# Top-k attention and a SwiGLU block in fp32: the `w_val` product by seven quarter products, and the transposed exp kept in the buffer of exp

## The chip, the cores and the metric

The kernel runs on one core of a Trainium2 chip. The metric is the device time of one execution in microseconds; the figure of the kernel before is the median of three runs. One more execution was recorded by the hardware profiler, and every row below is from it.

Names used throughout: PE is the matmul engine (PEld its weight loads), DVE the vector engine, ACT the scalar engine, POOL the GpSimd engine, SP the engine that issues most DMAs. Each takes its instructions in order. SBUF is the on-chip memory, PSUM the banks that PE writes its results to.

## The reference

```python
# attention: q, k, v are (8, 8, 576, 64), all fp32
scores = scale * np.matmul(q, k.transpose(0, 1, 3, 2))
kth = np.partition(scores, -32, axis=-1)[..., -32:-31]
scores = np.where(scores >= kth, scores, -1e9)
scores = scores - np.max(scores, axis=-1, keepdims=True)
attn = np.exp(scores)
attn = attn / (np.sum(attn, axis=-1, keepdims=True) + 1e-9)
attn_out = np.matmul(attn, v)
# the heads side by side: x is (4608, 512)
x = attn_out.transpose(0, 2, 1, 3).reshape(4608, 512)
# w_gate, w_val: (512, 1536); w_out: (1536, 512)
g = x @ w_gate
out = (g / (1 + np.exp(-g)) * (x @ w_val)) @ w_out
```

## The kernel before

**Attention** goes in 160 units: for each of 8 batches, 5 tiles of queries (four of 128, the last of 64), and 4 pairs of heads. A unit of the first four tiles has two heads of 576 scores in each of 128 rows; in the last tile both heads share the rows, and a unit is half the work (128x576 instead of 128x1152). So a batch is 20 units, 16 full ones and 4 halves. One unit passes through these helpers:

- `scores` (L278): PE multiplies query and key into four PSUM banks (two for a half), ACT copies them to `sc` (L313, L299).
- `select` (L316): DVE finds the 32nd largest score by four rounds of `max` and three of `match_replace` (L329, L333), then writes a mask into `e` (L339).
- `penalize` (L343): POOL makes `bias` (L349) and adds `sc` to `e` (L351).
- `weigh` (L354): ACT's exp with the row sums (L360). `normalize` (L368): DVE's reciprocal, ACT scales `e` (L375).
- `turn` (L377): PE transposes `e` in nine 128x128 chunks into PSUM (L387), ACT copies them to a tile `et` (L388). `values` (L403): PE multiplies `et` with `v` (L407, L416), ACT copies the result to the block's `xT` (L431).

**The feed-forward part** goes in 18 blocks of 256 rows (`feed`, L457). A block has six pairs of chunks of 128 columns of `w_gate` and `w_val`. For a pair, `product` makes a gate product and a value product, each 2 chunks x 4 matmuls of 128x256 (L471) into one PSUM bank (`ps_f`, 3 buffers). After the gate, ACT makes tanh, half and add (L496 to L498) and POOL a product (L499); after the value, ACT copies (L503) and POOL multiplies into `h` (L504). Then the product with `w_out`: in block 0 as it stands (L517), in the others already by seven quarter products (`quarter`, L545; matmuls L557), for which POOL makes sums and differences of the quarters of `h` (L564, L572, L577, L605) and of the results (L543). Their weights `T[1]` to `T[7]` are made once by POOL, at the end of `weights` (L125).

**Weights** come in 36 pieces during the first 190 us, each rounded by ACT, DVE and POOL (`rounded`, L103).

**What sets the order.** The main loop (L729) is written out by hand. In step n it puts out, in this order: what is left on the queue `on_act`, `penalize(n-1)`, the queue `on_pool`, `turn(n-3)`, `values(n-4)`, the matmuls of `scores(n+1)`, `weigh(n-1)`, the copies of these scores, and DVE's rounds of `select(n)`, with pieces of the feed-forward part between them (`pieces`, L702). How many pieces a unit gets is a credit, `share(n)` (L689): `beside` (6.4) less what the unit's other PE work costs, in units of 4 matmuls of 128x256. `product` charges 2 a product, a `quarter` 1.5, so a block of seven quarter products costs 34.5. `product` does not emit its ACT part: it puts a function on `on_act`, which in turn puts one on `on_pool`; `piece` (L661) empties each as soon as it holds two, and the main loop at fixed places. The last lines (L793 on) bind PE, DVE, ACT and POOL to the order written; SP's DMAs are ordered by the scheduler. A block starts when all its rows of `xT` are done, and the last two blocks run when attention is over.

Of the kernel before, what the change touches and what calls it, by code (L numbers as in the profile page):

```python
# [9 lines left out]
ALU = mybir.AluOpType  # L10
FP32 = mybir.dt.float32
# [4 lines left out]
P = 128  # L16
# [4 lines left out]
BLK = 256  # L21
# [4 lines left out]
def kernel(  # L26
# [35 lines left out]


    nc = tc.nc
    B, H, S, D = q.shape
# [18 lines left out]
    conv = ctx.enter_context(tc.tile_pool(name="conv", bufs=2))  # L84
    ffn = ctx.enter_context(tc.tile_pool(name="ffn", bufs=2))
    ps_t = ctx.enter_context(tc.tile_pool(name="ps_t", bufs=5, space=PSUM))
    ps_f = ctx.enter_context(tc.tile_pool(name="ps_f", bufs=3, space=PSUM))

    ident = consts.tile([P, P], FP32, name="ident")
    make_identity(nc, ident[:])  # L90
    NV = 4
    vlast = []
# [32 lines left out]
    def weights():  # L125
# [66 lines left out]
        T[3] += [wo[:, MQ + m, hi] for m in range(MQ)]  # L192
        yield

    ready = [0]
    early = [lambda: None]
    plain_done = []
    T = {i: [] for i in range(1, 8)}
# [178 lines left out]
    def turn(n):  # L377

        last = units[n][1] == J
        e = state[n].pop("e")  # L380
        et = work.tile([P, 2 * J + 1, P], FP32, tag="et", name="et")
        for c0, cn in ((0, J), (J, 1)) if last else ((0, J), (J, 1), (J + 1, J)):
            ps = ps_t.tile([P, 512], FP32, tag="t", name="etps")
            kl = R if last and c0 == J else P
            for c in range(cn):
                k0 = (c0 + c) * P
                nc.tensor.transpose(ps[0:kl, c * P : (c + 1) * P], e[:, k0 : k0 + kl], ident[:])  # L387
            nc.scalar.copy(  # L388
                et[0:kl, c0 : c0 + cn, :],
                ps[0:kl, 0 : cn * P].rearrange("p (c j) -> p c j", c=cn),  # L390
            )
            if c0 == J:
                yield
        state[n]["et"] = et
# [62 lines left out]
    def feed(kb):  # L457
# [4 lines left out]
        x = xT.pop(kb)  # L462
        hs = []

        def product(w, s, then):
            ps = ps_f.tile([P, 2, BLK], FP32, tag="f", name="f")
            need(4 * s + (2 if w is wg else 4))
            for i in range(2):
# [11 lines left out]
                yield 1  # L480

        plain = kb == 0
        first, late = slice(0, P), slice(P, BLK)
# [5 lines left out]
        for s in range(MS):  # L489
            h = ffn.tile([P, 2, BLK], FP32, tag="h", name="h", bufs=MS + 1)  # L490
            hs.append(h)


            def gate(ps, h=h):
                half = ffn.tile([P, 2, BLK], FP32, tag="gv", name="half_g", bufs=3)
                nc.scalar.activation(h[:], ps[:], AF.Tanh, scale=0.5)  # L496
                nc.scalar.mul(half[:], ps[:], 0.5)
                nc.scalar.add(h[:], h[:], 1.0)  # L498
                on_pool.append(lambda: nc.gpsimd.tensor_mul(h[:], h[:], half[:]))  # L499

            def value(ps, h=h, s=s):
                val = ffn.tile([P, 2, BLK], FP32, tag="gv", name="val", bufs=3)
                nc.scalar.copy(val[:], ps[:])  # L503
                on_pool.append(lambda: nc.gpsimd.tensor_mul(h[:], h[:], val[:]))  # L504

            yield from product(wg, s, gate)
            yield from product(wv, s, value)
        o = ffn.tile([P, 2, DM], FP32, tag="o", name="o", bufs=1)
# [31 lines left out]
        x_ps = ps_f.tile([P, 2, DH], FP32, tag="f", name="x_ps")  # L540

        def tt(out, in0, in1):
            nc.gpsimd.tensor_tensor(out, in0, in1, ALU.add)  # L543

# [35 lines left out]
        yield from quarter(5, x_ps[:, 0])  # L580
        a = ffn.tile([P, 2, DH], FP32, tag="gv", name="p57", bufs=3)

# [4 lines left out]
        on_act.append(keep_x)  # L587
        b = ffn.tile([P, 2, DH], FP32, tag="gv", name="p16", bufs=3)

# [99 lines left out]
    def share(n):  # L689
# [8 lines left out]

        beside = 6.4 if T[1] else 7.0
        return beside * n_heads(units[n][1]) / 2 - others  # L700
# [136 lines left out]
```

## Time and profile before

| what | us |
|---|---|
| median of three runs | 1822.87 (1821.8 to 1823.49) |
| the profiled execution | 1821.36 |
| its span, first to last instruction | 1819.6 |
| PE busy | 1702.6 (94%) |
| DVE busy | 1603.0 (88%) |
| ACT busy | 1219.7 (67%) |
| POOL busy | 1036.1 (57%) |
| matmuls of the gate product, L471, 1728 records | 401.6, 382 ns each |
| matmuls of the value product, L471, 1728 records | 399.1, 382 ns each |
| POOL `e + sc`, L351, 160 | 382.8, 2393 ns each |
| POOL `h` products, L499 and L504, 108 each | 138.2 and 139.7 |
| DMA | 59.65 MB, mean 33 GB/s |

An fp32 matmul of the program stands in the trace as two records, one behind the other. The length of a record (382 ns) is longer than the distance at which such records follow each other, since matmuls are pipelined; rates are read from a run of records in the timeline. A wait in the profile is put down to what came last, and idle time of an engine that isn't the bottleneck costs nothing by itself.

### The profile page before, as it was taken

The numbers are of one execution on the slowest core, as the hardware profiler recorded it, in microseconds if no ns is written. First come the engines' busy times: TensorE is split into PE (matmuls) and PEld (weight loads), VectorE is DVE, ScalarE is ACT, GpSimd is POOL, SyncE is SP. The second block draws the span as 40 slices with busy tenths as digits, with TensorE's granted clock in tenths as the row PEclk, the third lists the DMA queues.
The fourth block names the chain that finished last, engine by engine and source line by source line (L and its number), as shares of the span: only waits on it lengthen the run. The fifth ranks groups of instructions, "written<-read, shape, count | busy, mean of one in ns | idle before, by whom it ended". The sixth has DMA issues, their size and how long they took to land.

```text
span 1819.6 us, 30520 instructions
## 1 busy us (share of the span) xinstructions
PE 1702.6 (94%) x10756; PEld 1406.1 (77%) x10756; DVE 1603.0 (88%) x3372; ACT 1219.7 (67%) x2977; POOL 1036.1 (57%) x930
## 2 busy tenths in 40 slices
PE   3447999899999999999999999999999999999999
PEld 2336768687788788887888878887888878888887
DVE  7999999999999799997999989998999989998400
ACT  6788666677667576666767676767676766675532
POOL 5878656555565646554465646564556554646354
PEclk7668999999999999999999999999999999999999
DMA  7433030002100030000300021000300011000000
GB/s 195 132 95 103 3 86 8 12 1 48 47 1 13 2 76 17 13 1 19 76 13 1 12 56 39 1 13 3 74 19 13 1 36 32 1 13 12 1 12 12
DMA packets 109305, 59.65 MB, mean 33 GB/s; under 512 B 88544, under 2 KB 96992, under 8 KB 109152
## 3 DMA queue, kind: packets, MB, share of 16 engines
q1 hardware_dynamic: 108016, 57.37, 12.1%
q8 instruction: 85, 1.39, 0.3%
q14 instruction: 68, 0.56, 0.1%
q10 hardware_dynamic: 1136, 0.33, 0.1%
HBM read 48.23 MB, written 9.44 MB: 32 GB/s over the span
## 4 chain that ended last, share of the span: by engine, by line
PE 88%; DVE 4%; ACT 4%; POOL 2%; issue 2%; DMA 1%; SPq 0%; POOLq 0%; DVEq 0%; ACTq 0%
PE f L471 42%; PE x_ps L557 9%; PE av L416 8%; PE etps L387 8%; PE s L308 8%; PE y_ps L557 7%; PE s L294 2%; DVE rest L333 2%; PE av L407 2%; DVE m L329 1%; PE o_ps L517 1%; PE kqps L263 1%; ACT e L360 1%; DVE e L339 1%; ACT e L375 1%
## 5 line engine op out<-in xcount | busy, mean ns | idle before, releaser
L329 DVE MAX8 m<-rest 128x8 f32<-128x576 f32 x864 | 612.7, 744 | 2.2
L351 POOL TENSOR_TENSOR e<-e,sc 128x1152 f32<-128x1152 f32 (+1 forms) x160 | 382.8, 2393 | 87.5 <-DVE e L339 73.1
L333 DVE MATCH_REPLACE8 rest<-m,rest 128x576 f32<-128x576 f32 x576 | 423.0, 739 | 0.0
L471 PE MATMUL f<-xT,wg 128*128 128x256 f32 x1728 | 401.6, 382 | 0.0
L471 PE MATMUL f<-xT,wv 128*128 128x256 f32 x1728 | 399.1, 382 | 0.0
L471 PEld LDWEIGHTS f<-xT,wg 128*128 128x128 f32 x1728 | 323.0, 190 | 62.8 <-issue 21.5
L471 PEld LDWEIGHTS f<-xT,wv 128*128 128x128 f32 x1728 | 324.4, 190 | 58.8 <-issue 16.6
L499 POOL TENSOR_TENSOR h<-h,half_g 128x512 f32<-128x512 f32 x108 | 138.2, 1279 | 293.6 <-ACT h L498 293.3
L329 DVE MAX8 m<-sc 128x8 f32<-128x576 f32 x288 | 205.0, 747 | 103.7 <-ACT sc L299 56.9
L360 ACT ACTIVATE e<-e,bias 128x576 f32<-128x576 f32 x288 | 222.1, 777 | 80.6 <-POOL e L351 80.5
L387 PE MATMUL etps<-ident,e 128*128 128x128 f32 (+1 forms) x1312 | 184.0, 285 | 90.9 <-issue 32.3
L388 ACT COPY et<-etps 128x512 f32<-128x512 f32 (+1 forms) x448 | 184.4, 484 | 124.6 <-PE etps L387 123.5
L387 PEld LDWEIGHTS etps<-ident,e 128*128 128x128 f32 (+1 forms) x1312 | 158.4, 146 | 118.0 <-issue 38.4
L504 POOL TENSOR_TENSOR h<-h,val 128x512 f32<-128x512 f32 x108 | 139.7, 1294 | 184.5 <-ACT val L503 184.4
L375 ACT ACTIVATE e<-e,tot 128x576 f32<-128x576 f32 x288 | 211.9, 790 | 1.5 <-DVE tot L372 1.5
L333 DVE MATCH_REPLACE8 rest<-m,sc 128x576 f32<-128x576 f32 x288 | 211.5, 740 | 0.0
L308 PE MATMUL s<-kqT 64*128 64x288 f32 x1024 | 172.3, 449 | 9.1 <-ACT kqT L268 8.8
L339 DVE TENSOR_SCALAR e<-sc,m 128x576 f32<-128x576 f32 x288 | 173.3, 637 | 3.4
L416 PE MATMUL av<-et,v 128*64 128x128 f32 (+1 forms) x2560 | 171.4, 279 | 0.0
L313 ACT COPY sc<-s 128x288 f32<-128x288 f32 x512 | 164.3, 403 | 2.5 <-PE s L308 2.5
L496 ACT ACTIVATE h<-f 128x512 f32<-128x512 f32 x108 | 65.4, 605 | 132.9 <-PE f L471 132.9
L416 PEld LDWEIGHTS av<-et,v 128*64 128x64 f32 x2560 | 134.9, 143 | 22.7 <-issue 6.8
(73 smaller groups left out, 2021.1 us busy)
## 6 DMA issues: line engine op xcount, KB each, us to landing
v<-in_v_dram SPq DMA_DIRECT2D x32, 256.0 KB, 3.0
kq_in<-in_k_dram SPq DMA_DIRECT2D x63, 128.0 KB, 2.8
kq_in<-in_q_dram SPq DMA_DIRECT2D x63, 128.0 KB, 2.9
w<-in_moe_w_gate_dram SPq DMA_DIRECT2D x12, 512.0 KB, 3.7
w<-in_moe_w_val_dram SPq DMA_DIRECT2D x12, 512.0 KB, 3.8
w<-in_moe_w_out_dram SPq DMA_DIRECT2D x12, 512.0 KB, 3.6
out_dram<-o SPq DMA_DIRECT2D x38, 128.0 KB, 2.4
out_dram<-o SPq DMA_DIRECT2D x16, 256.0 KB, 2.4
```

Of the source, the lines that this page charges most:

```text
L308: nc.tensor.matmul(ps[:, 0:half], slab[d, q0 : q0 + P], slab[d, k0 : k0 + half])
L329: nc.vector.max(m[:, t, 8 * r : 8 * r + 8], cur[:, hs])
L333: nc.vector.match_replace(rest[:, hs], m[:, t, 8 * r : 8 * r + 8], cur[:, hs], LOWEST)
L339: nc.vector.tensor_scalar(e[:, hs], sc[:, hs], m[:, t, TOP_K - 1 : TOP_K], FAR, ALU.is_lt, ALU.mult)
L351: nc.gpsimd.tensor_tensor(e[:, every], e[:, every], sc[:, every], ALU.add)
L360: nc.scalar.activation(e[:, hs], e[:, hs], AF.Exp, bias=bias[:, t : t + 1], scale=scale, accum_out=tot[:, t : t + 1],)
L375: nc.scalar.mul(e[:, hs], e[:, hs], tot[:, t : t + 1])
L387: nc.tensor.transpose(ps[0:kl, c * P : (c + 1) * P], e[:, k0 : k0 + kl], ident[:])
L388: nc.scalar.copy(et[0:kl, c0 : c0 + cn, :], ps[0:kl, 0 : cn * P].rearrange("p (c j) -> p c j", c=cn),)
L416: nc.tensor.matmul(av[hh * R : (hh + 1) * R, 0:ql], v_last[:, hh, :] if c == J else vt[:, hh, c, :], moving, start=last and c == 0, stop=c ...
L471: nc.tensor.matmul(ps[:, i, :], w[:, kc, m * P : (m + 1) * P], x[:, kc, :], start=(kc == 0), stop=(kc == KC - 1),)
L557: nc.tensor.matmul(ps, lhsT, T[i][m], start=m == 0, stop=m == MQ - 1)
```

## The change

1. **Value product.** In blocks 2 to 17 the value product of a pair of chunks goes by seven quarter products. `w_val` is cut in halves by rows (`c` 0-1 and 2-3) and by the two chunks of the pair, `x` in halves by rows and by its 256 columns. Each quarter product is two matmuls of 128x128. Four of them go into one PSUM tile (`f6157`), three into a second (`f234`). ACT copies both; POOL puts the four quarters of the result together by four additions (`sum_up`) and multiplies them into `h`. Block 0 and block 1 keep the old product.
2. **Sums of `x`.** At the start of a block POOL makes four differences `t1` to `t4` of the quarters of `x`.
3. **Sums of `w_val`.** They are made once, after block 1's value products, by POOL (four operations a pair; one of them overwrites a quarter of `wv`), written to DRAM (256 KB and 128 KB a pair), and read back for every pair of every block: `s12` has two buffers in SBUF, `s4` one. A fetch is issued for the pair after next (`s12`) or the next pair (`s4`).
4. **Transposed exp.** `turn` writes the transposed chunks back into the tile `e` that they were read from; the tile `et` is gone.
5. **Buffers and share.** `h` has 6 buffers (7 before), the tiles of the tag `gv` 4 (3 before). A quarter-product value costs 1.75 (2 before), and `beside` is 6.25 (6.4 before).

```diff
-    NV = 4
+    NV, NG = 4, 4
...
+        while not plain_v:
+            yield
+        for s in range(MS):
+            c0 = 2 * s * P
+            a11, a12 = (wv[:, i : i + 2, c0 : c0 + P] for i in (0, 2))
+            a21, a22 = (wv[:, i : i + 2, c0 + P : c0 + 2 * P] for i in (0, 2))
+            s12, s4 = sums_tiles()
+            nc.gpsimd.tensor_tensor(s12[:, 0], a21, a22, add)
+            nc.gpsimd.tensor_tensor(s12[:, 1], s12[:, 0], a11, sub)
+            nc.gpsimd.tensor_tensor(s4[:], a12, s12[:, 1], sub)
+            nc.gpsimd.tensor_tensor(a21, a11, a21, sub)
...
+            nc.sync.dma_start(kept[0][:], s12[:].rearrange("p a c m -> p (a c m)"))
+            nc.sync.dma_start(kept[1][:], s4[:].rearrange("p c m -> p (c m)"))
+            sv.append(kept)
+            yield
...
+    def fetch_s12(s):
+        t = ffn.tile([P, 2, 2, P], FP32, tag="s12", name="s12", bufs=2)
+        nc.sync.dma_start(t[:].rearrange("p a c m -> p (a c m)"), sv[s][0][:])
+        return t
...
-        et = work.tile([P, 2 * J + 1, P], FP32, tag="et", name="et")
+        et = e[:].rearrange("p (c j) -> p c j", j=P)
...
+        quick = kb >= 2
+        if quick:
+            while len(sv) < MS:
+                next(weight)
+            if not coming:
+                coming.extend([fetch_s12(0), fetch_s12(1)])
+                coming4.append(fetch_s4(0))
...
+            for out_, in0, in1 in ((t1, b12, b11), (t2, b22, t1), (t3, b22, b12), (t4, b21, t2)):
+                nc.gpsimd.tensor_tensor(out_, in0, in1, ALU.subtract)
...
+        def quick_value(s, h):
...
+            s12, s4 = coming.pop(0), coming4.pop()
+            ps = ps_f.tile([P, 4, P], FP32, tag="f", name="f6157")
+            for i, (a, b) in enumerate((
+                (s12[:, 1], t2), (w[:, 0:2, 0], b11), (s12[:, 0], t1), (w[:, 0:2, 1], t3)
+            )):
+                for c in range(2):
+                    nc.tensor.matmul(ps[:, i], a[:, c], b[:, c], start=c == 0, stop=c == 1)
+            more = s + 1 < MS or kb + 1 < NBLK
+            if s + 2 < MS or kb + 1 < NBLK:
+                coming.append(fetch_s12((s + 2) % MS))
+            p = []
+
+            def keep():
+                p.append(ffn.tile([P, 4, P], FP32, tag="gv", name="p6157", bufs=NG))
+                nc.scalar.copy(p[0][:], ps[:])
+
+            on_act.append(keep)
+            yield 1
+            ps2 = ps_f.tile([P, 3, P], FP32, tag="f", name="f234")
+            for i, (a, b) in enumerate((
+                (w[:, 2:4, 0], b21), (s4, b22), (w[:, 2:4, 1], t4)
+            )):
+                for c in range(2):
+                    nc.tensor.matmul(ps2[:, i], a[:, c], b[:, c], start=c == 0, stop=c == 1)
+            if more:
+                coming4.append(fetch_s4((s + 1) % MS))
+
+            def combine():
+                q = ffn.tile([P, 4, P], FP32, tag="gv", name="val", bufs=NG)
+                nc.scalar.copy(q[:, 0:3], ps2[:])
+
+                def sum_up():
+                    u = p[0][:, 0:1]
+                    tt(q[:, 3], p[0][:, 2], p[0][:, 3])
+                    tt(u, u, p[0][:, 1:2])
+                    tt(q[:, 0:3], q[:, 0:3], p[0][:, 1:4])
+                    tt(q[:, 1:4], q[:, 1:4], u.to_broadcast([P, 3, P]))
+                    nc.gpsimd.tensor_mul(h[:], h[:], q[:].rearrange("p a t -> p (a t)").rearrange("p (r t) -> p r t", r=2))
+
+                on_pool.append(sum_up)
+
+            on_act.append(combine)
+            yield 0.75
...
-            h = ffn.tile([P, 2, BLK], FP32, tag="h", name="h", bufs=MS + 1)
+            h = ffn.tile([P, 2, BLK], FP32, tag="h", name="h", bufs=MS)
...
-            yield from product(wv, s, value)
+            if quick:
+                yield from quick_value(s, h)
+            else:
+                yield from product(wv, s, value)
+        if kb == 1:
+            plain_v.append(True)
...
-        beside = 6.4 if T[1] else 7.0
+        beside = 6.25 if T[1] else 7.0
```

More of the change, by code (lines that the diff above doesn't have):

```diff
@@ L85 @@
     ffn = ctx.enter_context(tc.tile_pool(name="ffn", bufs=2))
+    dram = ctx.enter_context(
+        tc.tile_pool(name="dram", bufs=1, space=bass.MemoryType.DRAM)
+    )
     ps_t = ctx.enter_context(tc.tile_pool(name="ps_t", bufs=5, space=PSUM))
@@ L193, in weights, with sums_tiles, fetch_s4 @@
         yield
+        while not plain_v:
[9 more added lines that the diff above has]
+            nc.gpsimd.tensor_tensor(a21, a11, a21, sub)
+            kept = (
+                dram.tile([P, 4 * P], FP32, tag=f"s12_{s}", name="s12_kept"),
+                dram.tile([P, 2 * P], FP32, tag=f"s4_{s}", name="s4_kept"),
+            )
+            nc.sync.dma_start(kept[0][:], s12[:].rearrange("p a c m -> p (a c m)"))
+            nc.sync.dma_start(kept[1][:], s4[:].rearrange("p c m -> p (c m)"))
+            sv.append(kept)
+            yield
+    sv, coming, coming4 = [], [], []
+    def sums_tiles():
+        return (
+            ffn.tile([P, 2, 2, P], FP32, tag="s12", name="s12", bufs=2),
+            ffn.tile([P, 2, P], FP32, tag="s4", name="s4", bufs=1),
+        )
+    def fetch_s12(s):
+        t = ffn.tile([P, 2, 2, P], FP32, tag="s12", name="s12", bufs=2)
+        nc.sync.dma_start(t[:].rearrange("p a c m -> p (a c m)"), sv[s][0][:])
+        return t
+    def fetch_s4(s):
+        t = ffn.tile([P, 2, P], FP32, tag="s4", name="s4", bufs=1)
+        nc.sync.dma_start(t[:].rearrange("p c m -> p (c m)"), sv[s][1][:])
+        return t
     ready = [0]
     early = [lambda: None]
-    plain_done = []
+    plain_done, plain_v = [], []
     T = {i: [] for i in range(1, 8)}
@@ L463, in feed @@
         hs = []
+        quick = kb >= 2
[5 more added lines that the diff above has]
+                coming4.append(fetch_s4(0))
+            b11, b12 = (x[:, 0:2, i : i + P] for i in (0, P))
+            b21, b22 = (x[:, 2:4, i : i + P] for i in (0, P))
+            t1, t2, t3, t4 = (
+                tx[:, i]
+                for tx in [ffn.tile([P, 4, 2, P], FP32, tag="tx", name="tx", bufs=1)]
+                for i in range(4)
+            )
+            for out_, in0, in1 in ((t1, b12, b11), (t2, b22, t1), (t3, b22, b12), (t4, b21, t2)):
+                nc.gpsimd.tensor_tensor(out_, in0, in1, ALU.subtract)
         def product(w, s, then):
@@ L480, in product, with tt @@
                 yield 1
+        def quick_value(s, h):
+            w = wv[:, :, 2 * s * P : 2 * (s + 1) * P].rearrange(
+                "p c (r m) -> p c r m", r=2
+            )
+            s12, s4 = coming.pop(0), coming4.pop()
[35 more added lines that the diff above has]
+            yield 0.75
+        def tt(out, in0, in1):
+            nc.gpsimd.tensor_tensor(out, in0, in1, ALU.add)
         plain = kb == 0
@@ L489, in feed @@
         for s in range(MS):
-            h = ffn.tile([P, 2, BLK], FP32, tag="h", name="h", bufs=MS + 1)
+            h = ffn.tile([P, 2, BLK], FP32, tag="h", name="h", bufs=MS)
             hs.append(h)
             def gate(ps, h=h):
-                half = ffn.tile([P, 2, BLK], FP32, tag="gv", name="half_g", bufs=3)
+                half = ffn.tile([P, 2, BLK], FP32, tag="gv", name="half_g", bufs=NG)
                 nc.scalar.activation(h[:], ps[:], AF.Tanh, scale=0.5)
@@ L501, in value @@
             def value(ps, h=h, s=s):
-                val = ffn.tile([P, 2, BLK], FP32, tag="gv", name="val", bufs=3)
+                val = ffn.tile([P, 2, BLK], FP32, tag="gv", name="val", bufs=NG)
                 nc.scalar.copy(val[:], ps[:])
@@ L540, in feed @@
         x_ps = ps_f.tile([P, 2, DH], FP32, tag="f", name="x_ps")
-        def tt(out, in0, in1):
-            nc.gpsimd.tensor_tensor(out, in0, in1, ALU.add)
         def quarter(i, ps):
@@ L580, in feed @@
         yield from quarter(5, x_ps[:, 0])
-        a = ffn.tile([P, 2, DH], FP32, tag="gv", name="p57", bufs=3)
+        a = ffn.tile([P, 2, DH], FP32, tag="gv", name="p57", bufs=NG)
         def keep_x():
@@ L587, in feed @@
         on_act.append(keep_x)
-        b = ffn.tile([P, 2, DH], FP32, tag="gv", name="p16", bufs=3)
+        b = ffn.tile([P, 2, DH], FP32, tag="gv", name="p16", bufs=NG)
         def keep_y():
```

## The prediction

> **What bounds the kernel now.** I read the page first: its busy line, the shares of the chain that ended last, then the stretches of 210 us (about a batch of 20 units each) and the waits.
>
> ```profile
> PE 1702.6 (94%) x10756; PEld 1406.1 (77%) x10756; DVE 1603.0 (88%) x3372; ACT 1219.7 (67%) x2977; POOL 1036.1 (57%) x930
> ...
> PE 88%; DVE 4%; ACT 4%; POOL 2%; issue 2%; DMA 1%; SPq 0%; POOLq 0%; DVEq 0%; ACTq 0%
> ```
>
> PE carries 88% of the chain. POOL looks free at 57%. The stretches say more: columns are the stretch, its length, then busy us of PE, PEld, DVE, ACT, POOL; the last row is the end, where attention is over.
>
> ```profile
> 840.00:1050.00 210.00, 207.17 (x1336) 172.49 (x1335) 196.48 (x415) 144.01 (x355) 115.22 (x104) 0.99 0.10 24
> 1260.00:1470.00 210.00, 208.23 (x1365) 172.58 (x1363) 200.15 (x416) 145.16 (x363) 120.63 (x111) 1.00 0.10 24
> 1690.00:1820.00 130.00, 124.79 (x698) 107.68 (x696) 15.53 (x31) 43.89 (x93) 59.02 (x64) 0.99 0.04 9
> ```
>
> In the middle PE is busy for 207 to 208 of 210 us and DVE for 196 to 200. So PE sets the pace, and DVE is only 5% behind: the most that the middle (some 1,450 us after block 1) can give before DVE sets it is about 5%. In the last 130 us PE works alone. The next view is the waits.
>
> ```profile
> POOL h L499 <- ACT h L498: 293.3, 85, 9.5
> POOL h L504 <- ACT val L503: 184.4, 55, 9.3
> ...
> ACT e L360 <- POOL e L351: 80.5, 37, 4.9
> POOL e L351 <- DVE e L339: 73.1, 37, 8.9
> ```
>
> POOL waits for ACT's copies, and sat idle for DVE ahead of only 37 of its 160 additions `e + sc` (L351). Many of the others start late, because POOL was still at the block's `h` products. POOL is in order, so its idle 43% is not free to whoever stands behind a waiting product. That is the place this change loads.
>
> **PE: what the quarter products save.** The built order has 8 matmuls of 128x256 for `w_val` in a pair of chunks, each standing twice in the trace (1728 records for 864): 16 records. After, 7 products x 2 = 14 matmuls of 128x128, 28 records. The rates are in the timeline (start, length, then the row).
>
> ```profile
> 1005.51 0.39 PE L407 MATMUL av<-et,vlast 128*128 128x128 f32 x2
> ...
> 1032.59 3.62 PE L471 MATMUL f<-xT,wg 128*128 128x256 f32 x16
> ```
>
> One 128x256 record lasts 0.379, so the 16 start (3.62-0.379)/15 = 0.216 us apart. L407 has 128 columns and full 128x128 weights, like the new products: 0.39 less one record's 0.275 leaves 0.112 between the two. A pair of chunks falls from 16 x 0.216 = 3.46 to 28 x 0.112 = 3.14, by 0.32 us. Sixteen blocks (2 to 17) of 6 pairs make 96: **-30.7 us**, 3.8 of it in the last two blocks. The bounds: 0.108 (half of 0.216) gives -41; if every weight load (0.190) stood bare, 28 x 0.190 = 5.32 gives +179. I take the L407 row, since its second load ran beside its first matmul; that only two records follow each other there is the open point.
>
> That open point has a rule against it. The Trainium skill, TensorE: Matmul & The Clock Gate, section "Part 3: Packing small matmuls", says that a weight load overlaps a running matmul only where the row group differs. The L407 records have the same row group and stand 0.112 apart, so the trace disagrees. By the rule, with 0.108 of load in front of 0.112 of matmul, a pair would cost some 6.2 us and the change would lose 260 us; this estimate enters no sum.
>
> **POOL: what is added.** Timeline rows give 128x256 in 0.70 start to start (2.09 for three) and 128x512 in 1.24, so about 0.42 for 128 elements and 0.97 for 384, which have no row (between 0.2 and 0.70, and between 0.70 and 1.24). Each pair adds two of each, 2.8 us (1.8 to 3.9); each block adds four subtractions for `t1` to `t4`, 2.8 us; once, 24 instructions of 0.69 make the sums of `w_val`, 16.6 us. In all 96 x 2.8 + 16 x 2.8 + 16.6 = 330 us: POOL goes from 1036 to about 1365 us, 75%. ACT copies 512 and 384 elements in place of 512: +0.40 a pair, 38 us, at 68% of its time.
>
> Where does this reach the path? Three places.
>
> (1) *The end of the products in a block.* Quarter 5 needs L572's sums of `h`, and these stand behind the last pair's product. The last block shows it:
>
> ```profile
> 1797.14 2.09 POOL L564 TENSOR_TENSOR xT<-h 128x256 f32<-128x256 f32 x3
> 1799.19 1.27 POOL L504 TENSOR_TENSOR h<-h,val 128x512 f32<-128x512 f32 x1
> 1800.41 2.09 POOL L572 TENSOR_TENSOR h<-h 128x256 f32<-128x256 f32 x3
> ...
> 1802.66 2.75 PE L557 MATMUL x_ps<-wo,h 128*128 128x256 f32 x12
> ```
>
> L572 ends at 1802.50 and quarter 5 starts at 1802.66: just in time. Four more additions put it 2.8 us later, bare, in each of the last two blocks. In the earlier blocks a unit of attention often stands between, with POOL's `e` too. Going through the built order block by block, PE has 8.7 us of cover against 11.0 us of POOL work in six of them, 8.5 against 12.2 in one and 6.2 against 8.2 in one; the rest are covered. Before, cover and work were about equal at worst. Sum: 6 x 2.3 + 3.7 + 2.0 + 2 x 2.8 = **+25 us** (0 to 35).
>
> (2) *Making the sums.* 16.6 us of POOL in one go at block 2, with the `e` of two units behind them, and PE waiting for the write to DRAM and the read back. A unit's scores are copied one unit ahead, which covers: DVE's unit is 11 us, the way `e`, exp, copies of `sc` takes 2.8 + 1.9 + 1.15 = 5.9, so 5 us are free, and POOL's own spare in those units takes some: **+9 us** (0 to 19).
>
> (3) *The circle POOL-ACT-POOL.* ACT's exp waits for POOL's `e`; the copies of `sc`, then of the products, stand behind exp; POOL's `h` product waits for the copy; the next `e` stands behind it.
>
> ```profile
> 1026.81 2.64 POOL L351 TENSOR_TENSOR e<-e,sc 128x1152 f32<-128x1152 f32 x1
> 1029.40 1.28 POOL L499 TENSOR_TENSOR h<-h,half_g 128x512 f32<-128x512 f32 x1
> 1033.64 1.38 POOL L504 TENSOR_TENSOR h<-h,val 128x512 f32<-128x512 f32 x1 [2.96 <-ACT val L503]
> 1034.99 0.21 POOL L349 TENSOR_SCALAR bias<-m 128x2 f32<-128x2 f32 x1
> 1035.16 2.65 POOL L351 TENSOR_TENSOR e<-e,sc 128x1152 f32<-128x1152 f32 x1
> ```
>
> Once round is 8.35 us against DVE's unit of 11. After: one more copy (+0.40) and the two 384-element additions behind it (1.94) make 10.7; where the built order has tanh (1.6) and the normalisation (1.4) ahead of the second copy, 13.7. I added the rows of each unit's circle in the built order, leaving out waits for PE: 161 us in a batch before, 183 after, of DVE's 199. On average it still fits; unit by unit it doesn't always. Carrying the lag from unit to unit with 5 us free, DVE waits 28 us over the six middle batches (3 before). But DVE has 5% to spare where PE sets the pace, so I take half: **+14 us** (0 to 60, where PE's PSUM slots add to it, see below).
>
> **The rest, costed at nothing.** *PSUM*: three tiles a pair over three buffers; the next pair's gate needs this gate's tile copied within 16 + 12 records, 3.1 us (6.9 before). ACT needs 1.0 us for its two reads and in the rows starts 0.2 us after the product. If ACT is late this cover is gone, at up to 0.5 us a pair, 46 us. *Fetches*: `s4` has one buffer; SP issues its load when the last product with it is done, and a whole gate and four quarter products (3.45 + 1.79 = 5.2 us) stand before the next; 128 KB land in 2.8 to 3.0 us. In SP's built order no load or store ahead of a fetch is released later than the fetch itself, so PE, and all that is behind the waiting matmul, gets it in time; a store that POOL holds back would break this. Traffic goes from 60 to 100 MB, at 33 GB/s of the 195 that the first slice shows. *`et` in `e`*: the mask of unit n writes the buffer whose last reader is `av` of n-4, which PE does ahead of the scores that DVE waits for anyway. *`h` with 6 buffers*: the first tanh of a block follows quarter 3 on PE. *`gv`*: four buffers for three tiles a pair; ACT blocks if POOL falls a whole pair behind, part of (3). *`beside` 6.25*: a unit's share falls from 4.4 to 4.25 where a block falls from 34.5 to 33, so blocks keep pace with units.
>
> **Sum.** 1821.4 (span 1819.6 and 1.8 around it) - 30.7 + 25 + 9 + 14 = 1838.7. The profiled execution is 1.5 under the median of the runs, so **1840 us**.
>
> **Rivals.** *A, faster:* the PE saving lands and POOL's load hides. For it: PE is 88% of the chain, the circle's mean is 16 us under DVE's in a batch, attention often lies before quarter 5. Against it: the just-in-time row. It decides from where quarter 5 waits under 1 us a block and DVE's wait for `sc` doesn't grow; then 1821.4 - 30.7 + 9 + 1.5 = **1801** (to 1815 with some stalls). *B, no change:* stalls and DVE eat just the saving, **1822** (1816 to 1829). *C, much slower:* the circle, not PE, sets the pace; ACT late, PSUM slots late: + 28 + 46 in place of 14, **1900** (from 1870). For it: many `e` start late already. Against it: 183 under 199. That the products aren't changed at all is excluded by the built order: 576 matmuls, 472 POOL operations, 204 DMAs more.
>
> **Numbers.** Forecast (1829 to 1870) 0.45, A 0.29, B 0.13, C 0.13. About 0.2% (3.6 us) is what can be told from no change. Faster: A and 0.03 of B, 0.32; same: 0.08 of B; slower: 0.45 + 0.13 + 0.02 of B = 0.60. The range reaches from A with all of its saving, 1795, to C's price, 1900, as both signs hold much; the likeliest case alone is 1829 to 1870.
>
> **What would show it.** Quarter products 0.11 apart in runs of 16 and 12, else the first term falls. POOL near 1365 us. A wait of quarter 5's PE records for POOL `h` near 25 us in all. DVE's wait for `sc` above today's 103 us by 15 to 40. If PE waits on the fetched sums, or on ACT's copies of `f`, in the hundreds, the terms that I set to nothing are wrong.

## The result: slower by 3.5%

The changed kernel takes 1886.77 us (median of four runs, 1885.92 to 1887.8); the kernel before took 1823.18 us on the same chip. The ratio is 1.0351, with a 95% interval from 1.0336 to 1.0366: 63.6 us are lost. The forecast was 1840. Its direction came true; it took the loss for 17 us. The measured time lies in the range of rival C (from 1870), but what C gave as the cause was not found (see the account by steps). One of the four executions of `a_spread` (experiment 4) ran at a granted clock of 0.649 and took 2486 us; its figures are those of the other three.

The page of the changed kernel: the busy line, the granted clock in 40 slices, and the shares of the chain that ended last.

```profile
PE 1694.9 (90%) x11908; PEld 1427.4 (76%) x11908; DVE 1643.7 (87%) x3372; ACT 1257.9 (67%) x3073; POOL 1372.9 (73%) x1402
...
PEclk7668999799999999999999999999999999999989
...
PE 63%; POOL 18%; ACT 11%; DVE 6%; issue 2%; DMA 1%; SPq 0%; POOLq 0%; ACTq 0%; DVEq 0%
```

POOL is where it was put (1365 forecast, 1372.9 found), yet its share of the chain went from 2% to 18%, and PE's from 88% to 63%. DVE, whose work was not touched, is busy for 40 us longer. The stretches (length, then busy us of PE, PEld, DVE, ACT, POOL, the clock, DMA) show where PE stands still:

```profile
840.00:1050.00 210.00, 200.03 (x1461) 169.36 (x1460) 192.72 (x394) 145.75 (x364) 153.20 (x160) 0.99 0.18 46
1260.00:1470.00 210.00, 202.90 (x1513) 173.25 (x1512) 199.70 (x413) 149.41 (x372) 162.63 (x173) 1.00 0.20 52
1750.00:1884.00 134.00, 122.29 (x804) 108.16 (x802) 17.52 (x37) 48.16 (x103) 92.29 (x112) 0.96 0.14 36
```

Before, PE was busy for 207 to 208 of 210 us; now for 200 to 203. At the end, where attention is over, it stood idle for 5.2 of 130 us before and stands idle for 11.7 of 134 now. The waits (who waits for whom: us in all, how many, the longest) of the changed kernel:

```profile
POOL h L613 <- ACT h L612: 131.2, 56, 9.2
...
DVE e L383 <- PE av L461: 57.5, 14, 12.7
...
DVE m L373 <- ACT sc L357: 40.0, 34, 9.6
...
DVE m L373 <- ACT sc L343: 35.3, 19, 6.7
...
PE etps L432 <- ACT e L419: 30.7, 14, 4.6
...
PE f L554 <- POOL tx L524: 16.3, 9, 4.6
...
PE y_ps L673 <- POOL xT L693: 12.6, 1, 12.6
...
PE x_ps L673 <- POOL h L688: 11.3, 8, 1.7
...
PE x_ps L673 <- POOL xT L680: 9.3, 4, 2.7
...
PE x_ps L673 <- POOL h L721: 5.1, 5, 1.3
```

and two of the kernel before that were not shown:

```profile
DVE m L329 <- ACT sc L299: 56.9, 15, 10.6
...
DVE m L329 <- ACT sc L313: 46.6, 28, 9.9
...
PE etps L387 <- ACT e L375: 10.9, 8, 4.6
```

POOL's long waits for ACT have shrunk (293 us ahead of the gate's product to 131): part of its spare time is used up. In their place PE waits for POOL in five rows: the differences of `x` (`tx`), the burst of sums (one wait of 12.6), and the first and the second sums of `h` and the later ones (`x_ps`, 25.7 in all; about 1 before). It waits 20 us more for ACT's scaled exp. DVE's wait for `sc` did **not** grow: 103.5 before, 75.3 now.

**An account by PE.** From the trace's records one can add up, from 243 us (in the first unit of the second batch) to the end, the time that no PE record covers, and, after 200 us, the time in which PE was busy while the granted clock stood at half; of this half is lost. With PE's saving this gives the difference of the spans to within 7 us in each of these runs, though nothing in it is fitted (the saving itself is the forecast's; experiment 7 measures a like one):

| run (span less that of before) | PE work | PE idle | busy at half clock, half of it | sum |
|---|---|---|---|---|
| changed kernel (+64.9) | -30.7 | +72.7 | +18.4 | +60.4 |
| sums and differences mended, `a_fixed` (+45.3) | -30.7 | +55.2 | +15.3 | +39.8 |
| the same kernel once more, `a_fixed_no_adds` (+38.3) | -30.7 | +54.7 | +8.5 | +32.5 |
| the same without additions, `a_fixed_free` (+8.0) | -30.7 | +25.2 | +12.3 | +6.8 |
| the same, last pair as before, `a_five` (+9.5) | -25.6 | +20.3 | +8.0 | +2.7 |
| first three pairs, `a_half` (+0.9) | -15.4 | +11.7 | -0.2 | -3.9 |
| last three pairs, `a_late` (+32.1) | -15.4 | +35.8 | +5.2 | +25.6 |
| before, with POOL additions, `b_pool_adds` (+42.8) | 0 | +31.9 | +4.6 | +36.5 |
| before, with less PE work, `b_less_pe` (-38.4) | -41.5 | +0.1 | +2.0 | -39.4 |

So most of the loss is PE standing still, and in the changed kernel a quarter as much again is PE at half speed. Eight of the nine sums fall short, by 1 to 7 us; that rest is in neither column. (The clock's part scatters: two profiles of one kernel differ by 7 us in it.)

### The profile page after: what moved, and what is told of

The parts are those of the page before. It is cut to its first block, busy times and chain, and to the rows that moved or that the text cites. A ratio compares the mean times of both kernels' runs of the same rounds, so it can differ in the third digit from the quotient of the medians.

```text
span 1884.5 us, 33865 instructions
## 1 busy us (share of the span) xinstructions
PE 1694.9 (90%) x11908; PEld 1427.4 (76%) x11908; DVE 1643.7 (87%) x3372; ACT 1257.9 (67%) x3073; POOL 1372.9 (73%) x1402
## 4 chain that ended last, share of the span: by engine, by line
PE 63%; POOL 18%; ACT 11%; DVE 6%; issue 2%; DMA 1%; SPq 0%; POOLq 0%; ACTq 0%; DVEq 0%
PE f L532 19%; PE f L554 8%; PE av L461 7%; PE etps L432 6%; PE f L571 6%; PE s L352 5%; PE x_ps L673 5%; POOL e L395 4%; ACT e L404 3%; POOL val L594 3%; PE y_ps L673 3%; DVE rest L377 2%; DVE m L373 2%; ACT sc L357 2%; POOL p L594 2%
## 5 line engine op out<-in xcount | busy, mean ns | idle before, releaser
L532 PEld LDWEIGHTS f<-xT,wg 128*128 128x128 f32 x1728 | 318.8, 191 | 61.2 <-issue 23.1
L433 ACT COPY e<-etps 128x512 f32<-128x512 f32 (+1 forms) x448 | 184.2, 484 | 183.8 <-PE etps L432 183.4
L432 PE MATMUL etps<-ident,e 128*128 128x128 f32 (+1 forms) x1312 | 188.9, 290 | 107.8 <-ACT e L419 30.7
L383 DVE TENSOR_SCALAR e<-sc,m 128x576 f32<-128x576 f32 x288 | 212.5, 773 | 60.1 <-PE av L461 57.5
L432 PEld LDWEIGHTS etps<-ident,e 128*128 128x128 f32 (+1 forms) x1312 | 162.3, 150 | 132.6 <-ACT e L419 37.8
L594 POOL TENSOR_TENSOR val<-val,p 128x384 f32<-128x384 f32 x192 | 195.5, 1018 | 45.4 <-ACT val L577 37.0
L461 PE MATMUL av<-e,v 128*64 128x128 f32 (+1 forms) x2560 | 174.3, 282 | 0.0
L461 PEld LDWEIGHTS av<-e,v 128*64 128x64 f32 x2560 | 137.3, 146 | 23.1 <-issue 6.4
L554 PE MATMUL f<-tx,s 128*128 128x128 f32 x768 | 120.8, 280 | 16.3 <-POOL tx L524 16.3
L352 PEld LDWEIGHTS s<-kqT 64*128 64x128 f32 x1024 | 95.9, 197 | 47.6 <-issue 17.6
```

The lines of the kernel that those rows point to most:

```text
L352: nc.tensor.matmul(ps[:, 0:half], slab[d, q0 : q0 + P], slab[d, k0 : k0 + half])
L383: nc.vector.tensor_scalar(e[:, hs], sc[:, hs], m[:, t, TOP_K - 1 : TOP_K], FAR, ALU.is_lt, ALU.mult)
L461: nc.tensor.matmul(av[hh * R : (hh + 1) * R, 0:ql], v_last[:, hh, :] if c == J else vt[:, hh, c, :], moving, start=last and c == 0, stop=c ...
L532: nc.tensor.matmul(ps[:, i, :], w[:, kc, m * P : (m + 1) * P], x[:, kc, :], start=(kc == 0), stop=(kc == KC - 1),)
L554: nc.tensor.matmul(ps[:, i], a[:, c], b[:, c], start=c == 0, stop=c == 1)
```

## Experiments

Times are medians, each with its ratio to the kernel before on the same chip (1822.4 to 1823.3 us) and the 95% interval of the ratio.

### 1. The transposed exp in `e`, alone

```diff
-        et = work.tile([P, 2 * J + 1, P], FP32, tag="et", name="et")
+        et = e[:].rearrange("p (c j) -> p c j", j=P)
```

> The kernel before with the transposed exp alone moved into the buffer of exp. Theory Q (POOL's added operations hold up its in-order queue, and through it ACT, PE and DVE) and theory P (POOL's added operations slow DVE's mask, which shares something with POOL: a mask took 507 ns beside an idle POOL and about 1000 ns beside a busy one) expect no change, within 4 us of 1823. Theory R (the mask of unit n now waits for av of unit n-4, so e starts late and everything behind it) expects 1835 to 1855 and a wait of the mask for PE av of 30 to 60 us, as in the changed kernel (57.5 us).

Measured: 1823.05 us, 1.0003 [0.9993, 1.0012].

```profile
DVE m L329 <- ACT sc L313: 46.4, 29, 9.0
DVE e L339 <- PE av L416: 41.2, 10, 9.6
...
DVE m L329 <- ACT sc L299: 26.2, 14, 6.7
```

The mask does wait for `av` now (41.2 us), but the wait for `sc` behind it falls by 31 us, to 72.6. This part costs nothing by itself, as predicted. Whether it costs something beside the other parts was not tried: there is no room for a tile `et` in the changed kernel.

### 2. Does POOL slow DVE's mask?

The mask (`e<-sc,m`) is the only part of DVE's work that got longer. The rows of the mask before and after, by its line: shortest, median and longest in ns.

```profile
L339 DVE TENSOR_SCALAR e<-sc,m x288: 490/509/2040, 24.2 to 1723.9; 128x576 f32<-128x576 f32 x144
```

```profile
L383 DVE TENSOR_SCALAR e<-sc,m x288: 489/520/2930, 24.2 to 1795.8; 128x576 f32<-128x576 f32 x144
```

A mask with no POOL operation beside it takes 505 to 507 ns in both kernels. Those with POOL at work throughout spread widely, from 495 to 2620 ns in the changed kernel, with a median of about 980 in both. `max` (747 ns alone, 743 beside POOL) and `match_replace` (740 and 739) do not care. The next two runs read and write the mask's operands in a strided order, on the kernel before and on the changed one:

```diff
-                e[:, hs], sc[:, hs], m[:, t, TOP_K - 1 : TOP_K], FAR, ALU.is_lt, ALU.mult
+                e[:, hs].rearrange("p (a b) -> p b a", a=2), sc[:, hs].rearrange("p (a b) -> p b a", a=2), m[:, t, TOP_K - 1 : TOP_K], FAR, ALU.is_lt, ALU.mult
```

> The kernel before with the mask walked through with a stride (same elements, two interleaved halves), meant to take DVE out of the mode that collides with POOL. Theory P expects one duration for all masks, 600 to 700 ns, with and without POOL beside it, so DVE's sum of 183 us stays within 15 us and the time within 5 us of 1823. If all masks stay in two groups (about 507 and about 1000 ns), the stride doesn't take away the collision and the experiment on the changed kernel says nothing.

> The changed kernel with the same strided mask. Theory P: the mask's sum falls from 212 us to 175 to 200 us and the time falls by as much as DVE gains or more, to 1850 to 1875. Theory Q: DVE isn't what ends last, the time stays within 6 us of 1887.

Measured: 1834.62, 1.0063 [1.0046, 1.008], and 1907.19, 1.0461 [1.0445, 1.0476]. The busy lines of the first and of the second:

```profile
PE 1707.5 (93%) x10756; PEld 1407.8 (77%) x10756; DVE 1649.2 (90%) x3372; ACT 1221.2 (67%) x2977; POOL 1054.5 (58%) x930
```

```profile
PE 1700.2 (89%) x11908; PEld 1429.7 (75%) x11908; DVE 1686.2 (88%) x3372; ACT 1260.6 (66%) x3073; POOL 1395.3 (73%) x1402
```

The stride did not remove the collision: a mask alone takes 728 ns, beside POOL about 1220 on average (median about 1170). So, as the first expectation says of this case, the run on the changed kernel decides nothing between the theories. What the two runs give instead is a price: 46 us more of DVE cost 11.7 us on the kernel before, 42 us more cost 20.4 on the changed one (POOL grew by 18 and 22 us with it). By this price, an estimate, the 40 us by which the mask got longer stand for some 10 to 20 of the 94 us that were lost on the way (63.6 and the saving of 30.7).

### 3. Without the four additions

```diff
-                    tt(q[:, 3], p[0][:, 2], p[0][:, 3])
...
-                    nc.gpsimd.tensor_mul(h[:], h[:], q[:].rearrange("p a t -> p (a t)").rearrange("p (r t) -> p r t", r=2))
+                    nc.gpsimd.tensor_mul(h[:], h[:], p[0][:].rearrange("p a t -> p (a t)").rearrange("p (r t) -> p r t", r=2))
```

> The changed kernel without POOL's four additions a pair: h is multiplied by the first copied tile instead of the assembled value, so the output is not the reference's; PE, ACT, the fetches and the buffers are as in the changed kernel. POOL falls by about 265 us, to 1110. Theories P and Q both expect most of the loss back: the added 63.6 us plus the 30.7 us that PE saves, less the sums made once (18) and the differences of x (15): 1825 to 1845. If theory R carries the loss it stays above 1865.

Measured: 1851.41, 1.0157 [1.0142, 1.0172], above the 1825 to 1845 that were expected; the mask is back at 172.9 us. The additions carry 35 us. Without them the kernel is still 28 us slower than before, and DVE's waits are not shorter (132.8 us in the changed kernel, 138.4 here):

```profile
DVE m L373 <- ACT sc L357: 56.1, 44, 10.1
DVE e L383 <- PE av L461: 55.9, 13, 12.0
...
DVE m L373 <- ACT sc L343: 26.4, 13, 6.7
```

### 4. The sums of `w_val` in small steps; the differences of `x` earlier; both

`a_spread` makes one operation of the sums at a time between other work, from the time when the weights are there. `a_tx_early` makes the differences of `x` for the next block at the end of a block, where its rows are done. `a_fixed` does both.

```diff
             nc.gpsimd.tensor_tensor(s12[:, 0], a21, a22, add)
+            yield
+            yield
             nc.gpsimd.tensor_tensor(s12[:, 1], s12[:, 0], a11, sub)
...
+        if kb >= 1 and kb + 1 < NBLK and done.get(kb + 1, 0) == NHP * BLK:
+            make_tx(kb + 1, xT[kb + 1])
```

> The changed kernel with the sums of w_val made one operation at a time, from the moment the other sums of weights are there, and only the six in-place ones after block 1's value products. The burst of 24 operations at 320 to 338 us, PE's idle 12.7 us in it and the 13.7 us at half clock after it should go. If the burst costs what the second batch shows (233.9 against 214.3 us), 15 to 22 us come back: 1865 to 1872. If that batch is late for the blocks' own reasons, under 6 us come back.

> The changed kernel with the four differences of x made during the last quarters of the block before, wherever the rows are already there. PE idles 17.7 us over the middle ahead of the first quarter product, waiting for them. If these stalls are on the path, and each of over 3 us brings a stretch of half clock with it, 15 to 25 us come back: 1862 to 1872. If another wait takes their place, under 8 us.

> Both edits together. If the parts add up: 1887 less the gains of the two kernels beside it, 1842 to 1857. POOL still does all of its additions, so theories P and Q (POOL's added operations as the rest of the loss) expect it to stay 25 us or more above the kernel before.

Measured: 1872.5, 1.0268 [1.0251, 1.0285]; 1879.21, 1.0307 [1.0291, 1.0322]; both 1861.24, 1.0206 [1.0189, 1.0223]. The run `a_fixed_no_adds` holds the same kernel as `a_fixed`, with all of its additions, and is a second measurement of it: 1865.63, 1.0238 [1.0221, 1.0255]. So I take 1863.4. The burst cost 14 us (forecast: 9), the late differences 7.6 us (forecast: nothing beyond their POOL time), together 23. Both single gains are below the 15 us and more that were expected before the runs, and of PE's 16.3 us of waits for `tx` the mended kernel keeps 8.6. The burst as PE saw it in the changed kernel (start, length, row, idle time before it):

```profile
320.65 2.75 PE L673 MATMUL x_ps<-wo,h 128*128 128x256 f32 x12
335.97 2.93 PE L673 MATMUL y_ps<-t,xT 128*128 128x256 f32 x6 [12.57 <-POOL xT L693]
338.69 2.13 PE L432 MATMUL etps<-ident,e 128*128 128x128 f32 x9
...
349.77 1.15 PE L432 MATMUL etps<-ident,e 128*128 128x128 f32 x9
```

The wait is not for the sums and their way through DRAM, as the forecast had it, but for three sums of `h` that stand behind 15 us of burst on POOL (24 operations from 320.30 us on, the sums of `h` at 335.20). And it costs more than itself: the nine transposes after it take 2.13 us, 11 us later 1.15. By the stretches the granted clock was 0.55 from 326 to 338 us, still 0.66 from 338 to 342, and 1.00 after.

### 5. The additions alone, on the kernel before; and the same time in memsets

`b_pool_adds` is the kernel of 1. with four additions a pair onto a scratch tile, ahead of the value product on `h`. `b_pool_sets` has five memsets in their place (and an addition of one element, so that they too wait for ACT's copy).

```diff
+                def more():
+                    if kb >= 2:
+                        q = ffn.tile([P, 4, P], FP32, tag="scr", name="scr", bufs=1)
...
+                        tt(q[:, 1:4], q[:, 1:4], q[:, 0:1].to_broadcast([P, 3, P]))
+                    nc.gpsimd.tensor_mul(h[:], h[:], val[:])
```

> The kernel before (with the transposed exp in the buffer of exp, which makes room and made no difference) with the four additions a pair on POOL in blocks 2 to 17, into a scratch tile that nobody reads: POOL's load of the change alone, without its products, copies, fetches and differences. Without the additions the changed kernel was 35 us faster (1851). Theories P and Q expect the same load to cost the kernel before 25 to 45 us: 1848 to 1868, with DVE's masks at 210 us. If the additions only hurt together with the new products, under 10 us.

> The kernel before with the transposed exp in e, and with POOL loaded ahead of each value product of blocks 2 to 17 as in the run with four additions a pair (1866.7 us, 43.7 over the same kernel without them), but by an operation that reads nothing: a one-element addition that waits for ACT's copy, then five memsets of 512 elements on a scratch tile (no such memset stands in a trace; by the memset of 128 at 0.20 us and a guessed fixed part of 0.1, some 2.6 us a pair; the length is to be read off). Theory Q (POOL is in order, and what stands behind the additions is late): the time is again 35 to 45 us over 1823, whatever the mask does. Theory P (the additions slow DVE's mask, and that sets the pace): the mask's group stays near 173 us and the time within 10 us of 1823. If memsets slow the mask as additions do (group near 199 us), the run tells nothing between the two.

Measured: 1866.73, 1.0241 [1.0225, 1.0258], and 1871.67, 1.027 [1.0255, 1.0286]. Lines of the page of the first and of the second:

```profile
L339 DVE TENSOR_SCALAR e<-sc,m 128x576 f32<-128x576 f32 x288 | 198.9, 727 | 47.5 <-PE av L416 45.1
```

```profile
L514 POOL MEMSET scr<- 128x512 f32 x480 | 260.2, 542 | 27.8
...
L339 DVE TENSOR_SCALAR e<-sc,m 128x576 f32<-128x576 f32 x288 | 191.5, 701 | 51.6 <-PE av L416 49.2
```

With 278 us of additions, POOL costs the kernel before 43.4 us; with 280 us of memsets and small additions, 48.9. The mask got longer by 25.6 us in the one and by 18.2 in the other. The cost goes with POOL's time and not with the mask's, which speaks for the queue. It isn't a clean separation, since memsets slow the mask too (a mask that starts with more than 250 ns of a memset to go has a median of 852 ns), and the expectation had called a mask near 199 us undecided. By the price of experiment 2 on this kernel, the mask would stand for some 5 to 7 us of either loss (an estimate).

### 6. The mended kernel without the additions

> The changed kernel with sums of w_val made in small steps, differences of x made in the block before, and without sum_up's four additions (h is multiplied by one tile of quarter products, so the output is not the reference's). If the three costs add: about 1863 (two measurements with the additions, 1861 and 1866) less 35 = 1828 us, still no faster than before, and then some 35 us are elsewhere (ACT's longer copies, PSUM, PE at half clock after its waits). If PE's half clock and its waits come from the three together (a wait that is short enough costs no clock): half clock after 200 us falls from 58 to about 25 us, and the time to 1795 to 1810, near what the prediction's rival A gave.

(The edits are those of 3. and 4. together.) Measured: 1828.86, 1.0032 [1.0021, 1.0042]. The costs add: 1863.4 less 34.5. So even without the additions, without the burst and with most of the differences made early, 35 to 36 us are missing against 1822.9 less 30.

### 7. Does PE set the pace at all?

At this point (with the first run of 8. known) I held that the saving could not arrive: 20 units in the middle took about 209 us in the kernel before, in `a_half`, and on average in `a_fixed_free`, whatever PE's work. `b_less_pe` leaves one of eight matmuls of the value product out, `b_less_pe2` two.

```diff
-                for kc in range(KC):
+                last = KC - 1 - (w is wv and kb >= 2 and i == 1)
+                for kc in range(last + 1):
```

> The kernel before with one of the eight matmuls of each w_val product left out in blocks 2 to 17 (the last quarter of the rows for the second chunk, so the output is not the reference's): 96 x 2 records x 0.216 = 41.5 us of PE less, and nothing else changed. If PE sets the pace of the middle, as the prediction took it: 1823 - 41 = 1782 us (DVE's 5% of room, some 70 us, is not used up). If the middle is held by attention's chain through DVE, with PE only equally late: the last two blocks give 2 x 6 x 0.43 = 5 us, the middle some 0 to 15, so 1803 to 1818 us, and PE's idle time in the middle grows by 25 us or more.

> The same with two of the eight matmuls left out: 83 us of PE less. If PE sets the pace until DVE does (70 us of room in the middle, 10 us from the last two blocks): 1740 to 1750 us. If the middle is held already: 10 us from the last blocks and little more than in the run with one left out, 1795 to 1812 us.

Measured: 1782.6, 0.9778 [0.9762, 0.9795], and 1755.26, 0.9631 [0.9617, 0.9645]. That idea falls: of 41.5 us less of PE, 39.8 arrive. Of 83, 67 do. The stretches of the second show what stops it:

```profile
840.00:1050.00 210.00, 205.28 (x1372) 169.96 (x1370) 207.01 (x437) 153.07 (x379) 120.44 (x109) 0.99 0.11 27
1260.00:1470.00 210.00, 207.21 (x1338) 171.18 (x1337) 208.17 (x439) 149.26 (x370) 124.37 (x113) 0.99 0.10 24
```

DVE is now busy for 207 to 208 of 210. The prediction's reading of the bound was right: PE sets the pace, and DVE takes over when some 70 us are gone.

### 8. Which pairs?

The mended kernel with quarter products in some pairs of a block only: the first three (`a_half`), the last three (`a_late`), the first, third and fifth (`a_even`), and all but the last (`a_five`).

```diff
-            if quick:
+            if quick and s < 3:
```

> The kernel with sums in small steps and early differences of x (1861 and 1866 us in two measurements), but quarter products only for the first three of the six pairs of a block; the last three are computed as before, so that the end of a block's products is as before. Output as the reference's. If the cost goes with the number of additions: half of +40 over the kernel before, about 1842 us. If it is the end of the products (place (1): the last pair's additions ahead of quarter 5): the saving is 15, the cost of the additions is hidden beside the three whole products, and the time is 1810 to 1820.

> As the run with quarter products in the first three pairs of a block (1824.8 us), but in the last three. Output as the reference's. If the cost goes with the number of additions, the same 1825 us. If it is the end of a block, where quarter 5 and the next stages wait for the last pair's additions: most of the difference between 1825 and the 1863 with all six, so 1845 to 1860 us.

> As the run with quarter products in the first three pairs of a block (1824.8 us), but in the first, third and fifth, so that a whole product and a gate stand between each two sets of additions. Output as the reference's. If additions cost where POOL gets no break between two sets: below 1824.8, 1808 to 1820 us, which would beat the kernel before. If they cost by their distance from the end of the block: between the first three (1825) and the last three (1856), 1830 to 1845 us.

> Quarter products in all pairs of a block but the last. Output as the reference's. Against 1863 with all six (1861 and 1866). If it is the last pair's additions alone that cost: its own 5 us of PE saving is given up and some 30 us of cost with it, 1830 to 1838 us. If cost goes with the number of additions, or POOL is behind by the fifth pair already: 1848 to 1860 us.

Measured: first three 1824.8, 1.001 [1.0, 1.0019]; last three 1856.13, 1.0182 [1.0163, 1.0201]; every second 1825.63, 1.0014 [1.0005, 1.0024]; all but the last 1830.12, 1.0039 [1.0024, 1.0054]. The same work costs 31 us more at the end of a block than at its start, and the sixth pair alone costs 33 us more than its saving of 5. The first three and every second came out between the two expectations of their runs, the last three and all but the last in the range that put the cost at the end of the block. The waits of PE's `w_out` products for POOL, in `a_fixed` and in `a_five`:

```profile
PE etps L444 <- ACT e L431: 30.8, 15, 4.7
...
PE x_ps L692 <- POOL h L707: 11.6, 8, 1.7
...
PE x_ps L692 <- POOL xT L699: 9.4, 4, 2.7
...
PE x_ps L692 <- POOL h L740: 5.8, 5, 1.3
```

```profile
PE etps L445 <- ACT e L432: 19.0, 13, 4.6
...
PE x_ps L693 <- POOL h L741: 2.2, 2, 1.4
...
PE x_ps L693 <- POOL xT L700: 0.6, 3, 0.2
```

26.8 us of waits fall to 2.8, and behind them 12 us of waits for the exp. How the last pair does it, in the last block of the changed kernel (POOL, then PE):

```profile
1860.46 2.10 POOL L680 TENSOR_TENSOR xT<-h 128x256 f32<-128x256 f32 x3
1862.51 0.46 POOL L594 TENSOR_TENSOR val<-p 128x128 f32<-128x128 f32 x1
1862.93 0.46 POOL L594 TENSOR_TENSOR p<-p 128x128 f32<-128x128 f32 x1
1863.34 2.07 POOL L594 TENSOR_TENSOR val<-val,p 128x384 f32<-128x384 f32 x2
1865.49 1.26 POOL L586 TENSOR_TENSOR h<-h,val 128x512 f32<-128x512 f32 x1
1866.71 2.09 POOL L688 TENSOR_TENSOR h<-h 128x256 f32<-128x256 f32 x3
```

```profile
1863.07 2.75 PE L673 MATMUL x_ps<-t,xT 128*128 128x256 f32 x12
1867.48 2.86 PE L673 MATMUL x_ps<-wo,h 128*128 128x256 f32 x12 [1.66 <-POOL h L688]
```

Between L680 and the product on `h` now stand 2.98 us of additions; PE waits 1.66 us, so 1.3 were covered.

No split beat the kernel before: a pair that is not the last costs 5.5 to 6.4 us over the 16 blocks and saves 4.9.

### 9. The second PSUM tile and the second copy, alone

```diff
+                if two and i == 1:
+                    ps2 = ps_f.tile([P, 2, BLK], FP32, tag="f", name="f2")
...
+                if i == 0:
+                    scr = ffn.tile([P, BLK], FP32, tag="scr", name="scr", bufs=1)
+                    nc.scalar.copy(scr[:], ps[:, 0])
+                nc.scalar.copy(val[:, i], ps[:, i])
```

> The kernel before with the transposed exp in e, and in blocks 2 to 17 each value product in two PSUM tiles, one for each chunk of 256 (three tiles a pair over three buffers, as after the change), with three copies of 256 elements in place of one of 512 (the third is a double onto a scratch tile; estimate 3 x 0.27 against 0.48 to 0.52 us, so +0.3 us of ACT a pair, where the change adds 0.4). PE's and POOL's work is that of before. If the unexplained 30 to 36 us are the copies and the PSUM tiles: 1845 to 1860 us. If these are hidden, as the prediction costed them: 1820 to 1828 us, and the rest stays open between the smaller waits.

Measured: 1826.95, 1.0021 [1.0012, 1.0031], with ACT busy for 1256.0 us, as in the changed kernel. Three tiles on three buffers and the longer copies cost the kernel before 4 us: nearly hidden, as the prediction had it.

## Why the prediction was wrong, step by step

| step | predicted | measured | by |
|---|---|---|---|
| quarter products on PE | -30.7 | about -29.5 | 39.8 of 41.5 arrive in `b_less_pe` |
| (1) end of the products | +25 | +38 | the sixth pair: 33.3, and the 4.9 it saves |
| (2) making the sums | +9 | +14 | `a_spread` |
| (3) circle POOL-ACT-POOL | +14 | not found | see below |
| differences of `x` | 0 | +8 to 9 | `a_tx_early`; the rest of 23.4 in `a_fixed` |
| the rest | 0 (and 1.5 of offset) | +32 | five pairs: 1830.1 less (1822.9 - 24.6) |

The measured column makes +62.5 to +63.5, against a loss of 63.6. It has to come out near it, since the rows are differences along one row of kernels (changed, mended, five pairs, before); the sum does not check them. The costs were forecast at 48 us and came to 92 to 93.

- **The step that failed most is the one that set everything outside the three places at nothing.** It measured 40 to 41 us. The differences of `x` were listed as 2.8 us of POOL a block, and no PE wait was looked for; yet the first quarter product needs `t2`, and POOL makes it as a block starts. In the longest row PE waits 4.6 us, and 8 to 9 us in all came back when they were made earlier where the rows were done. The other 32 us (35 by the two profiled executions) are spread: in `a_five`'s trace PE is idle 20 us longer (8 of it for the exp, 4 for `tx`) and loses 8 to the clock, and some 7 are in neither. Most of the items that the prediction did name show no such cost: PE waits for no fetch in the list, PSUM and copies cost 4 us, `et` in `e` nothing alone. `beside` is 6.25 in every kernel with quarter products and no run varies it, so the new share stays a possible part of the 32 us.
- **The saving was right.** Quarter products stand 0.112 us apart in runs of 16 and 12, as the L407 rows said (2574 intervals, median 0.112). PE sets the pace, and DVE has the room that was read.
- **(1) had the right mechanism and too small a size.** The prediction charged ten of the sixteen blocks, eight of them in part. Without the sixth pair 24 us of direct waits go, about what was forecast (the row of quarter 5 alone, `h L688`, was 11.3 in the changed kernel, not the 25 that were to show there; quarter 7 before it waits 9.3). With them go 12 us of waits for the exp, and some at half clock. What the prediction left out was what follows a wait: the unit behind it is late too, and PE may be at half speed.
- **(2) had the wrong wait.** The 9 us were to come from the sums' way through DRAM and the `e` behind them; the one long wait, 12.6 us, was for three sums of `h` behind the burst, and half clock followed it.
- **(3) did not show.** DVE's wait for `sc` should have grown by 15 to 40 us. It fell by 28 against the kernel before, and against the kernel of experiment 1, where the mask waits for `av` too, it is 75.3 after 72.6; both waits together are 133 there against 114. Without the additions they are 138, so it isn't the additions that raise them. The additions are worth 34.5 us in the mended kernel, and the sixth pair's place accounts for about as much; by this difference, if the costs add, next to nothing is left for those of the other five.
- **Rival C came near the time and not near the cause.** It held that the circle sets the pace and that PSUM slots come late, at 46 us: the circle did not show, the tiles cost 4 us on the kernel before, and 41.5 us less of PE gave 39.8.
- **DVE's mask was taken as fixed and isn't.** It got 40 us longer. The estimate of experiment 2 is 10 to 20 us in the changed kernel, and lies inside the terms above; no run separates it, since `a_no_adds` takes lateness and collision away together.
- **The end was not PE's alone.** The prediction read its last row as PE working alone; POOL is busy for 59 of those 130 us, for 92 of 134 now, and PE's idle time there went from 5 to 12 us.

What stays open: which of the small waits in the 32 us come from which part. The transposed exp in `e` together with late POOL work is one candidate that I could not try, the share another.

## What to carry to other kernels

An in-order engine's idle share is not room: ask what stands behind the added work where PE is about to need it. Here 3 us of additions a block, ahead of the products that PE waits for, were most of the 33 us that the last pair cost, and by the difference nearly nothing elsewhere. When an edit trades PE work for POOL work, price every first use by PE (of differences, of sums, of the last tile of a loop) as bare unless a row shows the cover, and add 2 to 3 us of half clock for each wait of about 4 us or more (after the six such waits of the changed kernel behind 200 us, 1.7 to 4.6 us were lost to it). If PE sets the pace, taking PE work away alone tells at once whether a saving can arrive; everything above that is cost.

## What was not expected of the hardware

- One DVE operation of three collides with POOL: the mask, one tensor and a scalar per row, goes from 507 ns to a median of about 980 with POOL at work throughout, and to 852 when it meets a memset early; `max` and `match_replace` stay within 1%. POOL pays too: in `b_pool_sets` a memset that takes 525 ns alone has a median of 782 when it starts within 300 ns behind a mask's start. The Trainium skill, SBUF — State Buffer, section "SBUF: two separate sides", says that DVE and GpSimd lock a shared pair of ports for a whole instruction, when DVE runs in a two-port mode or has two SBUF inputs. That the mask and POOL hold each other up fits. Its strided form, 728 ns alone, still took about 1220 beside POOL; no run here shows in which mode either form ran.
- The granted clock moves in the middle of a kernel whose PE is busy for 90% of the span. After a wait it is slow first and comes back 3.4 to 10 us later: in the kernel before, PE waits 4.63 us for the exp until 637.28, its nine transposes then take 1.99 us, and 8 us later 1.15; the mean clock is 0.57 from 637 to 641 us and 1.00 from 641. Busy time of PE at half clock, after 200 us: 17 us before the change, 54 after. The Trainium skill, TensorE: Matmul & The Clock Gate, section "Part 1: The HAM clock gate (the "warmup" mystery)", puts the window at about 3.4 us of idling to fall to half and as much of work to return. The length of the stretches, 3.4 us or multiples of it, agrees; the idling does not always: in the kernel before, half clock also followed waits of 1.96 us (at 344 us) and 2.40 (at 849 us).
